# A code path of its own for the last 129 to 160 rows of the largest expert, in an attention and mixture-of-experts kernel

## The chip, the cores and the metric

The kernel is one program on one core of a Trainium2 chip. The metric is the device time of one execution in microseconds. Before the change the median of three runs is 644.22 us (641.96 to 645.08).

## The reference

Three layers follow each other on 2304 tokens of width 512, all in float32: masked attention, one dense layer with a softmax-gated activation and a normalisation, and a mixture of eight experts of which each token uses one. The change touches only the third:

```python
def _moe2_ref(x, modality_id, w_gate, modality_bias, w1, w2):
    logits = x @ w_gate + modality_bias[modality_id]
    e_idx = np.argmax(logits, axis=1)
    logits_s = logits - logits.max(-1, keepdims=True)
    probs = np.exp(logits_s)
    probs /= probs.sum(-1, keepdims=True) + 1e-09
    gate_w = probs[np.arange(N), e_idx]
    for e in range(E):
        mask = e_idx == e
        h = np.maximum(x[mask] @ w1[e], 0.0)
        out[mask] = gate_w[mask, None] * (h @ w2[e])
```

Here `w1` is 8 x 512 x 1024 and `w2` is 8 x 1024 x 512. How many rows (tokens) an expert gets is known only on the chip, from the router's result. With the inputs of the runs the reference gives the eight experts 0, 0, 9, 0, 0, 4, 111 and 2180 rows; of the first 1536 tokens 1462 go to the expert with 2180.

## The kernel before, in words

**The order of the work.** Attention and the dense layer write the rows of the third layer's input to `y_d` in DRAM, and a router sorts the experts by size. The largest is the main expert (index 0), the others follow. Two pieces of 256 rows of the main expert run early, from the first twelve of the eighteen 128-token tiles (`EARLY_T`). The rest of its rows are counted in `n_r[0]`, 2180 - 512 = 1668 here, and run in pieces of 256, numbered j: piece 0 to 5 hold 256 rows each, piece 6 the last 132. Pieces 0 to 2 run between the small experts (`main_step`, `small`), pieces 3 to 6 in `rest(3)`, the last function of the program. All matrix products split a number into a high part (rounded float32, names ending in H) and a low part (L), and add three products: high x high, high x low, low x high.

**One piece of 256 rows, `chunk256` (L1040 ff).** The input rows are already gathered by GpSimd (`gather`, L982), transposed by TensorE (`transpose_x`, L134) and lie as `gH` and `gL`, 512 x 256, with the rows along the columns (the profile calls them xTH and xTL). The *up* part is 96 matmuls on L1055: 8 pieces of 128 of the 1024 hidden features x 4 chunks of the 512 inputs x 3 products. The stationary operand is a 128 x 128 tile of `w1`, the moving one 256 columns of the rows. After each 24 matmuls ScalarE (L1061, relu into `hH`) and VectorE (L1062, the low part into `hL`) empty a PSUM tile of 2 x 256 columns. Then `expert_out` runs once for each half of the rows, an *output block* of 128 rows: 8 chunks of the hidden features x 3 products = 24 matmuls on L1015, with 128 rows of `hH` or `hL` as the stationary operand and 512 columns of `w2` moving. ScalarE multiplies the sum by the rows' gate values (L1020), and GpSimd scatters the block's rows to their places in the output tensor (L1021, an indirect DMA; rows beyond the count have an index out of range and are dropped). Between the two blocks `then` transposes the rows of the next piece, whose gathers `ahead` has issued at the piece's start.

**Which code a piece runs (`rest`, `level`, L1284 to L1309).** The levels are nested branches on `n_r[0]`, taken on every engine. Level j asks whether rows are left (L1290, more than 256 j) and whether more than 128 are left (L1291). If so it runs `chunk256`, also when only 129 of the 256 rows exist; otherwise `chunk_few` (L1081), which is written for up to 128 rows.

**How the small experts end.** `chunk_few` closes its output in one of two ways. Up to 64 rows (`tiny`): the sum comes in two halves of 64 partitions, ScalarE copies one (L1153), VectorE multiplies the other (L1154) and adds the copy (L1155). Up to 128 rows: ScalarE does 256 of the columns (L1157), VectorE twice 128 (L1159). Either is followed by one scatter (L1160).

**What sets the order.** Each engine runs its instructions in the order of the program; a scheduler orders them when the program is built. Scatters and gathers are issued by GpSimd's queue, one after the other, and two scatters to `out` in one piece of code are ordered by the framework where they name the same tensor.

Of the kernel before, what the change touches and what calls it, by code (L numbers as in the profile page):

```python
# [28 lines left out]
def tile_attention_moe_moe2(  # L29
# [38 lines left out]
    HALF = DM // 2  # L68
    YA = HALF + NE
    TINY = P // 2  # L70
    EARLY = 2
    EARLY_T = 12
    NTC = NTILE + 2 * EARLY
# [966 lines left out]
    def chunk256(w, idx, j, side=(), ahead=None, then=None, loads=()):  # L1040
# [37 lines left out]
            then()  # L1078
        expert_out(w, idx, 2 * j + 1, slice(P, 2 * P), step, (1, 4))

    def chunk_few(w, idx, j, side=(), then=None, blk=0, tiny=False):  # L1081
        wH1, wL1, wH2 = w[:3]
        step, last = stepper(side)
# [63 lines left out]
            last[0] = then()  # L1147
        down(2)
        down(3)
        o = yo[0:n_, 0]  # L1150
        gate = idx[0:n_, 2 * j, 1:2].bitcast(F32)
        if tiny:
            nc.scalar.copy(yo[0:TINY, 1], p[TINY:])  # L1153
            nc.vector.tensor_scalar(o, p[0:TINY], gate, None, ALU.mult)  # L1154
            nc.vector.scalar_tensor_tensor(o, yo[0:TINY, 1], gate, o, ALU.mult, ALU.add)  # L1155
        else:
            nc.scalar.activation(o[:, 0:256], p[:, 0:256], AF.Copy, scale=gate)  # L1157
            for s_ in (slice(256, 384), slice(384, 512)):
                nc.vector.tensor_scalar(o[:, s_], p[:, s_], gate, None, ALU.mult)  # L1159
        nc.gpsimd.indirect_dma_start(  # L1160
            out=out[:, :], out_offset=indirect(idx[0:n_, 2 * j, 2:3].bitcast(U32)),
            in_=o, in_offset=None, bounds_check=NT - 1, oob_is_err=False)

    state = None
    done_att = False
# [104 lines left out]
    def more_chunks(w, i, j, cap, x, gathered=False):  # L1270
        if j >= cap:
            return
        with tc.If(n_r[i] > 256 * j):
# [7 lines left out]
            with big.Else():  # L1281
                chunk_few(w, idx[i], j)

    def rest(j, gathered=True):  # L1284
        cap = NT // 256

        def level(j, now, later, ready):
            if j >= cap:
                return
            with tc.If(n_r[0] > 256 * j):  # L1290
                with tc.If(n_r[0] > 256 * j + P) as big:  # L1291
                    def ahead():
                        if not ready:
                            gather(now, idx[0], j + 1)
                        if j + 2 < cap:
                            gather(later, idx[0], j + 2)

                    def then():
                        transpose_x(now)

                    if j + 1 < cap:
                        chunk256(W[0], idx[0], j, (), ahead, then)
                    else:
                        chunk256(W[0], idx[0], j)
                    level(j + 1, later, now, True)
                with big.Else():
                    chunk_few(W[0], idx[0], j)

        level(j, *xg, gathered)  # L1309

# [120 lines left out]
```

## Time and profile before

| | |
|---|---|
| median of three runs | 644.22 us |
| profiled execution | 643.14 us, its span in the trace 641.4 us |
| granted TensorE clock, mean | 0.986 of full speed |
| TensorE matmul (PE) busy | 602.3 us, 94% of the span |
| TensorE weight load (PEld) | 535.7 us, 84% |
| VectorE (DVE) | 346.8 us, 54% |
| ScalarE (ACT) | 286.3 us, 45% |
| GpSimd (POOL) | 151.5 us, 24% |
| the up matmuls of `chunk256` (L1055), all nine pieces | 3 x 288 matmuls, 81.8 + 82.0 + 81.4 us busy |
| the scatters of `chunk256` (L1021) | 14 shown, 14.1 us of GpSimd |

The busy times come from the hardware profiler on the core. Matmuls are pipelined: one begins before the end of the one ahead, so the length of a record (284 ns for 256 columns) is more than the distance from one start to the next. That distance is what counts for the time of a stream, and it is read from the start times in the list of instructions. A few records are missing from the trace (L1055 shows 864 matmuls, which is 9 x 96, and L1021 shows 14 of 18 scatters).

### The profile page before, as it was taken

How to read it: one execution, taken by the hardware profiler on the slowest of the kernel's cores; microseconds unless marked ns; L12 is line 12 of the kernel's file. 1: busy time of each engine (PE TensorE's matmuls, PEld its weight loads, DVE VectorE, ACT ScalarE, POOL GpSimd, SP SyncE). 2: the span in 40 equal slices, each digit the busy share in tenths (PEclk: the TensorE clock that was granted, in tenths of full speed). 3: DMA queues.
4: the chain of work that ended last, by engine and by line, in shares of the span. 5: the costliest groups of instructions: out<-in, count | busy, mean ns of one | idle time of the engine just before them, and what ended most of it. 6: DMA issues, size and time to landing. Idle time of an engine off the chain costs nothing. (4 is left out here: it accounts for less than half of the span.)

```text
span 641.4 us, 14417 instructions
## 1 busy us (share of the span) xinstructions
PE 602.3 (94%) x5546; PEld 535.7 (84%) x5546; DVE 346.8 (54%) x1020; ACT 286.3 (45%) x673; POOL 151.5 (24%) x223
## 2 busy tenths in 40 slices
PE   5887989999999999999999999999899999999992
PEld 4765777998889988978889999989798888899891
DVE  4865887488556775577488743217264643120120
ACT  3646675555554566557265522124335352221210
POOL 3652432112112352011023312310111203112101
PEclk9997989999999999999999999999999999999997
DMA  8676630224312123110044301445455453012010
GB/s 224 189 179 171 158 108 19 54 56 117 82 55 57 53 59 108 37 36 17 18 149 148 98 19 34 112 158 158 143 165 198 147 187 104 17 50 66 33 34 25
DMA packets 48387, 61.64 MB, mean 96 GB/s; under 512 B 29313, under 2 KB 32923, under 8 KB 48285
## 3 DMA queue, kind: packets, MB, share of 16 engines
q1 hardware_dynamic: 41421, 44.09, 24.7%
q0 software_dynamic: 4272, 11.57, 5.8%
q10 hardware_dynamic: 2592, 4.72, 2.0%
q8 instruction: 52, 0.85, 0.6%
q14 instruction: 50, 0.41, 0.2%
HBM read 48.40 MB, written 10.26 MB: 91 GB/s over the span
## 5 line engine op out<-in xcount | busy, mean ns | idle before, releaser
L1015 PE MATMUL py<-w2H,winL 128*128 128x512 f32 x288 | 92.1, 395 | 0.0
L1055 PE MATMUL pf<-xTL,w1H 128*128 128x256 f32 x288 | 81.8, 284 | 1.0 <-DVE xTL L994 1.0
L1055 PE MATMUL pf<-xTH,w1H 128*128 128x256 f32 x288 | 82.0, 285 | 0.0
L1055 PE MATMUL pf<-xTH,w1L 128*128 128x256 f32 x288 | 81.4, 283 | 0.0
L1062 DVE SCALAR_TENSOR_TENSOR winL<-pf,winL 128x512 fp32r<-128x512 f32 x36 | 24.9, 692 | 95.9 <-ACT winL L1061 95.8
L628 PE MATMUL ph<-winH,xTH 128*128 128x512 f32 x144 | 58.8, 408 | 4.2 <-DVE so L643 3.1
L1015 PEld LDWEIGHTS py<-w2H,winL 128*128 128x128 f32 x288 | 53.4, 188 | 10.5
L1061 ACT ACTIVATE winL<-pf 128x512 fp32r<-128x512 f32 x36 | 21.6, 599 | 87.5 <-PE pf L1055 87.5
L1055 PEld LDWEIGHTS pf<-xTL,w1H 128*128 128x128 f32 x288 | 56.2, 195 | 1.9 <-DVE xTL L994 1.6
L628 PE MATMUL ph<-winL,xTH 128*128 128x512 f32 x144 | 57.6, 400 | 0.0
L1055 PEld LDWEIGHTS pf<-xTH,w1H 128*128 128x128 f32 x288 | 56.1, 195 | 1.0 <-issue 0.5
L628 PE MATMUL ph<-winH,xTL 128*128 128x512 f32 x144 | 56.9, 401 | 0.0
L1055 PEld LDWEIGHTS pf<-xTH,w1L 128*128 128x128 f32 x288 | 56.2, 195 | 0.0
L1021 POOL DMA_INDIRECT out_dram<-yo,idx x14 | 14.1, 1007 | 142.6 <-ACT yo L1020 124.4
L687 PE MATMUL pa<-woH,nH 128*128 128x264 f32 x144 | 42.3, 293 | 1.0 <-ACT nH L676 1.0
L687 PE MATMUL pa<-woH,nL 128*128 128x264 f32 x144 | 42.6, 296 | 0.0
L687 PE MATMUL pb<-woH,nH 128*128 128x256 f32 x144 | 41.2, 286 | 0.0
L687 PE MATMUL pb<-woH,nL 128*128 128x256 f32 x144 | 41.0, 284 | 0.0
L687 PE MATMUL pa<-woL,nH 128*128 128x264 f32 x144 | 40.9, 284 | 0.0
L687 PE MATMUL pb<-woL,nH 128*128 128x256 f32 x144 | 40.8, 283 | 0.0
L462 POOL TENSOR_TENSOR ex<-ex,rd 72x288 f32<-72x288 f32 (+2 forms) x32 | 22.3, 696 | 70.9 <-DVE rd L457 44.4
L628 PEld LDWEIGHTS ph<-winH,xTH 128*128 128x128 f32 x144 | 27.4, 191 | 10.6 <-DVE so L643 4.5
(288 smaller groups left out, 1535.7 us busy)
## 6 DMA issues: line engine op xcount, KB each, us to landing
raw<-in_moe_w_dram SPq DMA_DIRECT2D x36, 512.0 KB
y_d<-yt ACTq DMA_DIRECT2D x18, 256.0 KB
raw<-in_moe_w_in_dram SPq DMA_DIRECT2D x8, 512.0 KB
raw<-in_moe_w_out_dram SPq DMA_DIRECT2D x8, 512.0 KB
qn<-in_q_dram SPq DMA_DIRECT2D x8, 288.0 KB
kn<-in_k_dram SPq DMA_DIRECT2D x8, 288.0 KB
vn<-in_v_dram SPq DMA_DIRECT2D x8, 288.0 KB
qn<-in_q_dram SPq DMA_DIRECT2D x16, 144.0 KB
```

The costliest lines, as they stand in the source:

```text
L462: nc.gpsimd.tensor_tensor(ex, ex, rd.unsqueeze(2).to_broadcast([nq, nt, nk]), ALU.mult)
L628: nc.tensor.matmul(ph, a[:, c, ts_], w[:, c, cs], start=n == 0, stop=n == 3 * KD - 1)
L687: nc.tensor.matmul(p, a[:, f], w[:, f, cols], start=n == 0, stop=n == 3 * KF - 1)
L1015: nc.tensor.matmul(p, a[:, f, s], x, start=n == 0, stop=n == 3 * KF - 1)
L1021: nc.gpsimd.indirect_dma_start(out=out[:, :], out_offset=indirect(idx[:, col, 2:3].bitcast(U32)), in_=o, in_offset=None, bounds_check=NT - ...
L1055: mm = nc.tensor.matmul(p[:, u], a[:, c, fs], x[:, c], start=n == 0, stop=n == 3 * KD - 1)
L1061: last[0] = (nc.scalar.activation(hH[:, f2s], p, AF.Relu), nc.vector.scalar_tensor_tensor(hL[:, f2s], p, 0.0, hH[:, f2s].bitcast(F32), ALU ...
L1062: nc.vector.scalar_tensor_tensor(hL[:, f2s], p, 0.0, hH[:, f2s].bitcast(F32), ALU.max, ALU.subtract))
```

## The change

A level whose rows number 129 to 160 (`TAIL`) runs a new function, `chunk_tail`, and no longer `chunk256`.

- Its up matmuls move 160 columns in place of 256, into the same PSUM tiles. ScalarE's relu works on 160 columns; VectorE writes the low part of the first 128 rows into `hL` as before and that of the other 32 behind the 160 columns of `hH`.
- The first output block keeps its 24 matmuls. The second, of up to 32 rows, has 16: per chunk of hidden features one with 64 stationary columns (32 rows high, the same 32 rows low) against the high part of `w2`, and one with 32 stationary columns (high) against its low part. The 16 stand between the two halves of the first block's 24.
- The second block's sum comes in two halves of 32 partitions and is closed by `add_two`: ScalarE copies one half, VectorE multiplies the other by the gate and adds the copy, into a buffer in `hid`. The first block is closed by `scale_split` (ScalarE 256 columns, VectorE twice 128). Each ends with a scatter, `add_two`'s first.
- `add_two` and `scale_split` are also what `chunk_few` now ends with; the tiny form stages its sum in `hid` where it used `yo`.
- In the levels the inner branch asks for more than 160 rows first, and falls through to `chunk256`; the other side asks for more than 128 (`chunk_tail`) or runs `chunk_few`. Each piece of 256 rows gives a hint for the next level's branch at its start (`hint_tail`).
- `chunk_tail` gathers and transposes no next piece.

```diff
--- before.py
+++ after.py
@@ -68,6 +68,8 @@
     HALF = DM // 2
     YA = HALF + NE
     TINY = P // 2
+    EXTRA = P // 4
+    TAIL = P + EXTRA
     EARLY = 2
     EARLY_T = 12
     NTC = NTILE + 2 * EARLY
@@ -1078,6 +1080,26 @@
             then()
         expert_out(w, idx, 2 * j + 1, slice(P, 2 * P), step, (1, 4))
 
+    def scatter_rows(o, idx, col, n):
+        nc.gpsimd.indirect_dma_start(
+            out=out[:, :], out_offset=indirect(idx[0:n, col, 2:3].bitcast(U32)),
+            in_=o, in_offset=None, bounds_check=NT - 1, oob_is_err=False)
+
+    def scale_split(idx, col, p):
+        o, gate = yo[:, 0], idx[:, col, 1:2].bitcast(F32)
+        nc.scalar.activation(o[:, 0:256], p[:, 0:256], AF.Copy, scale=gate)
+        for s_ in (slice(256, 384), slice(384, 512)):
+            nc.vector.tensor_scalar(o[:, s_], p[:, s_], gate, None, ALU.mult)
+        scatter_rows(o, idx, col, P)
+
+    def add_two(idx, col, p, n):
+        o = hid.rearrange("p q f -> p (q f)")[0:n, 0:2 * DM].rearrange("p (u d) -> p u d", u=2)
+        gate = idx[0:n, col, 1:2].bitcast(F32)
+        nc.scalar.copy(o[:, 1], p[n:2 * n])
+        nc.vector.tensor_scalar(o[:, 0], p[0:n], gate, None, ALU.mult)
+        nc.vector.scalar_tensor_tensor(o[:, 0], o[:, 1], gate, o[:, 0], ALU.mult, ALU.add)
+        scatter_rows(o[:, 0], idx, col, n)
+
     def chunk_few(w, idx, j, side=(), then=None, blk=0, tiny=False):
         wH1, wL1, wH2 = w[:3]
         step, last = stepper(side)
@@ -1147,19 +1169,47 @@
             last[0] = then()
         down(2)
         down(3)
-        o = yo[0:n_, 0]
-        gate = idx[0:n_, 2 * j, 1:2].bitcast(F32)
         if tiny:
-            nc.scalar.copy(yo[0:TINY, 1], p[TINY:])
-            nc.vector.tensor_scalar(o, p[0:TINY], gate, None, ALU.mult)
-            nc.vector.scalar_tensor_tensor(o, yo[0:TINY, 1], gate, o, ALU.mult, ALU.add)
+            add_two(idx, 2 * j, p, TINY)
         else:
-            nc.scalar.activation(o[:, 0:256], p[:, 0:256], AF.Copy, scale=gate)
-            for s_ in (slice(256, 384), slice(384, 512)):
-                nc.vector.tensor_scalar(o[:, s_], p[:, s_], gate, None, ALU.mult)
-        nc.gpsimd.indirect_dma_start(
-            out=out[:, :], out_offset=indirect(idx[0:n_, 2 * j, 2:3].bitcast(U32)),
-            in_=o, in_offset=None, bounds_check=NT - 1, oob_is_err=False)
+            scale_split(idx, 2 * j, p)
+
+    def chunk_tail(w, idx, j):
+        wH1, wL1, wH2 = w[:3]
+        for f2 in range(KF // 2):
+            p = ps.tile([P, 2, 256], F32, name="pf", tag="h")[:, :, 0:TAIL]
+            for u in range(2):
+                fs = slice(f2 * 256 + u, f2 * 256 + 256, 2)
+                n = 0
+                for c in range(KD):
+                    for a, x in ((wH1, gH), (wH1, gL), (wL1, gH)):
+                        nc.tensor.matmul(
+                            p[:, u], a[:, c, fs], x[:, c, 0:TAIL], start=n == 0, stop=n == 3 * KD - 1)
+                        n += 1
+            f2s = slice(2 * f2, 2 * f2 + 2)
+            nc.scalar.activation(hH[:, f2s, 0:TAIL], p, AF.Relu)
+            for dst, r in ((hL[:, f2s, 0:P], slice(0, P)), (hH[:, f2s, TAIL:TAIL + EXTRA], slice(P, TAIL))):
+                nc.vector.scalar_tensor_tensor(
+                    dst, p[:, :, r], 0.0, hH[:, f2s, r].bitcast(F32), ALU.max, ALU.subtract)
+        p = ps.tile([P, DM], F32, name="py", tag="y")
+        p2 = ps.tile([P, DM], F32, name="py", tag="y")
+
+        def down(f):
+            fl = dict(stop=f == KF - 1, skip_group_check=True)
+            nc.tensor.matmul(p, hH[:, f, 0:P], wH2[:, f], start=f == 0, **fl)
+            nc.tensor.matmul(p, hH[:, f, 0:P], lo2(w, f), start=False, **fl)
+            nc.tensor.matmul(p, hL[:, f, 0:P], wH2[:, f], start=False, **fl)
+
+        for f in range(KF // 2):
+            down(f)
+        for f in range(KF):
+            fl = dict(stop=f == KF - 1, skip_group_check=True)
+            nc.tensor.matmul(p2[0:2 * EXTRA], hH[:, f, P:P + 2 * EXTRA], wH2[:, f], start=f == 0, **fl)
+            nc.tensor.matmul(p2[0:EXTRA], hH[:, f, P:TAIL], lo2(w, f), start=False, **fl)
+        for f in range(KF // 2, KF):
+            down(f)
+        add_two(idx, 2 * j + 1, p2, EXTRA)
+        scale_split(idx, 2 * j, p)
 
     state = None
     done_att = False
@@ -1281,6 +1331,10 @@
             with big.Else():
                 chunk_few(w, idx[i], j)
 
+    def hint_tail(j):
+        tc.mark_branch_hint_location(
+            f"tail{j}", n_r[0] > 256 * j + TAIL, engines=mybir.ALL_ENGINES)
+
     def rest(j, gathered=True):
         cap = NT // 256
 
@@ -1288,7 +1342,7 @@
             if j >= cap:
                 return
             with tc.If(n_r[0] > 256 * j):
-                with tc.If(n_r[0] > 256 * j + P) as big:
+                with tc.If(n_r[0] > 256 * j + TAIL, preferred_fallthrough_block=True, label=f"tail{j}") as big:
                     def ahead():
                         if not ready:
                             gather(now, idx[0], j + 1)
@@ -1299,12 +1353,16 @@
                         transpose_x(now)
 
                     if j + 1 < cap:
+                        hint_tail(j + 1)
                         chunk256(W[0], idx[0], j, (), ahead, then)
                     else:
                         chunk256(W[0], idx[0], j)
                     level(j + 1, later, now, True)
                 with big.Else():
-                    chunk_few(W[0], idx[0], j)
+                    with tc.If(n_r[0] > 256 * j + P, preferred_fallthrough_block=True) as some:
+                        chunk_tail(W[0], idx[0], j)
+                    with some.Else():
+                        chunk_few(W[0], idx[0], j)
 
         level(j, *xg, gathered)
 
```

On GpSimd's queue the last piece (level 6 of `rest(3)`) read so before; xg_5954 is the buffer for a next piece's rows, and the names in brackets are what an instruction waits for (DMASW: the landing of an earlier indirect DMA).

```order
L1290 COMPARE_AND_BRANCH
L1291 COMPARE_AND_BRANCH
L982 DMA xg_5954<-y_d,idx_5945 128x512 [waits DMASW6_49,PE_49]
L982 DMA xg_5954<-y_d,idx_5945 128x512 [waits DMASW7_49,PE_49]
L1021 DMA out_dram<-yo,idx_5945 2304x512 [waits DMASW5_49,Activation_49]
L1021 DMA out_dram<-yo,idx_5945 2304x512 [waits DMASW0_49,Activation_49]
L1290 COMPARE_AND_BRANCH
```

With the change the same place, level 6's `chunk_tail`, reads:

```order
L1362 COMPARE_AND_BRANCH
L1084 DMA out_dram<-hid,idx_5945 2304x512 [waits DMASW7_49,DMASW6_49,DVE_49]
L1084 DMA out_dram<-yo,idx_5945 2304x512 [waits DMASW0_49,DMASW7_49,DVE_49,Activation_49]
L1345 ISA [waits DMASW4_49,DMASW5_49,DMASW3_49,DMASW6_49,DMASW2_49,DMASW1_49]
L1362 UNCONDITIONAL_BRANCH
```

The two gathers are gone. The second block's scatter (from `hid`) now comes first, and the first block's scatter (from `yo`), the last one of the program, waits for VectorE, for ScalarE and for DMASW7, which is the landing of the scatter ahead of it; before, the last scatter waited for ScalarE and for a DMA of an earlier time.

On TensorE's queue the new piece begins with the first four rows; the first two matmuls, which read the transposed rows, wait for PE's own count, ScalarE and VectorE. The last two rows are the last pair of 64 and 32 stationary columns.

```order
L1362 COMPARE_AND_BRANCH
L1186 MATMUL pf<-xTH,w1H 128x160 [waits PE_49,Activation_49]
L1186 MATMUL pf<-xTL,w1H 128x160 [waits DVE_49]
L1186 MATMUL pf<-xTH,w1L 128x160
...
L1207 MATMUL py<-w2H,winL 64x512 [waits DVE_49,Activation_49]
L1208 MATMUL py<-xTL,winL 32x512
```

The 96 up matmuls are followed by 12 of the first block, the 16 of 64 and 32 stationary columns, and 12 of the first block; the eight transposes that stood between the two blocks are not there.

## Rows read from the trace of the kernel before

**Rows 1.** Busy time by stretch, last piece: us, PE, PEld, DVE, ACT, POOL, PEclk, DMA, GB/s

```profile
605.78:629.30 23.52, 23.52 (x153) 21.12 (x151) 4.06 (x6) 4.84 (x8) 4.00 (x4) 1.00 0.16 47
```

**Rows 2.** Instructions in order of time, last piece: start us, us, engine, line, operation

```profile
605.78 0.28 PE L1055 MATMUL pf<-xTH,w1H 128*128 128x256 f32 x1
...
611.41 0.28 PE L1055 MATMUL pf<-xTH,w1L 128*128 128x256 f32 x1
...
612.21 0.71 PE L134 MATMUL px<-ident,xg 128*128 128x128 f32 x5
...
627.32 0.39 PE L1015 MATMUL py<-xTL,winL 128*128 128x512 f32 x1
...
628.91 0.39 PE L1015 MATMUL py<-w2H,winL 128*128 128x512 f32 x1
629.38 0.69 ACT L1020 ACTIVATE yo<-py,idx 128x512 f32<-128x512 f32 x1 [3.17 <-PEq L1290]
630.35 1.01 POOL L1021 DMA_INDIRECT out_dram<-yo,idx  x1 [2.83 <-ACTq L1290]
```

**Rows 3.** DMA queues from 620 to 642 us: packets, MB, share of 16 engines

```profile
q0 software_dynamic: 160, 0.27, 3.4%
```

**Rows 4.** Two lines' instructions at the end: count, min/median/max ns, first and last start

```profile
L1290 POOLq INC_SWDGE_SEM  x1: 1480/1480/1480, 630.7 to 630.7; - x1
```

```profile
L1426 POOLq DRAIN  x3: 46/109/5450, 635.1 to 641.1; - x3
```

**Rows 5.** The router in order of time, and weight loads by shape (busy us, mean ns)

```profile
111.91 1.03 PE L286 MATMUL pg<-wg,wt 128*128 128x8 f32 x8
```

```profile
L1055 PEld LDWEIGHTS pf<-xTH,w1L 128*128 128x128 f32 x288 | 56.2, 195 | 0.0
...
L134 PEld LDWEIGHTS px<-ident,xg 128*128 128x128 f32 x68 | 8.5, 140 | 2.1
L286 PEld LDWEIGHTS pg<-wg,wt 128*128 128x128 f32 x64 | 7.9, 192 | 0.8 <-ACT wt L283 0.4
```

**Rows 6.** A tiny expert's last matmuls, in order of time

```profile
534.60 0.40 PE L1126 MATMUL py<-woH,winL 128*128 128x512 f32 x1
534.84 0.39 PE L1128 MATMUL py<-woL,winL 128*64 128x512 f32 x1
```

**Rows 7.** The tiny expert's closing, in order of time, with idle time and releaser

```profile
535.31 0.58 ACT L1153 COPY yo<-py 64x512 f32<-64x512 f32 x1 [0.38 <-PE py L1128]
...
536.70 0.75 DVE L1155 SCALAR_TENSOR_TENSOR yo<-yo,idx 64x512 f32<-64x512 f32 x1
...
538.25 0.93 POOL L1160 DMA_INDIRECT out_dram<-yo,idx  x1 [2.72 <-DVE yo L1155]
```

**Rows 8.** Chain of waits from 600 us: the landings of two first-block scatters

```profile
603.13 2.73 DMA out_dram<-yo,idx
...
626.49 3.02 DMA out_dram<-yo,idx
```

**Rows 9.** Closing of the small expert of 111 rows, in order of time

```profile
467.01 0.40 PE L1131 MATMUL py<-woH,winL 128*128 128x512 f32 x1
...
467.44 0.47 ACT L1157 ACTIVATE yo<-py,idx 128x256 f32<-128x256 f32 x1 [0.30 <-DMA xg<-y_d,idx]
467.95 0.61 DVE L1159 TENSOR_SCALAR yo<-py,idx 128x128 f32<-128x128 f32 x2
```

```profile
469.37 1.02 POOL L1160 DMA_INDIRECT out_dram<-yo,idx  x1 [1.61 <-issue]
```

**Rows 10.** Branches on TensorE's queue: count, min/median/max ns, first and last start

```profile
L1290 PEldq COMPARE_BRANCH  x1: 65/65/65, 601.7 to 601.7; - x1
```

```profile
L1290 PEldq COMPARE_BRANCH  x6: 65/68/4557, 533.0 to 629.5; - x6
```

```profile
L1383 PEldq COMPARE_BRANCH  x4: 84/442/458, 452.1 to 532.5; - x4
```

**Rows 11.** Attention's plain float32 score matmuls, in order of time

```profile
121.31 0.68 PE L427 MATMUL bank<-kz,qT 128*72 128x72 f32 x8
```

## The prediction

> **What bounds the kernel now.** I read four views of the profile before the change, in this order. First the busy time by stretch: over the last piece, 605.78 to 629.30 us, TensorE is busy all 23.52 us at a granted clock of 1.00 while VectorE and ScalarE work 4 to 5 us of it [rows 1]. So in this piece a matmul saved is time saved, up to the point where the closing work takes over. Second the instructions in order of time [rows 2]: the first up matmul starts at 605.78, the 48th at 611.41, so one starts every 5.63 / 47 = 0.1198 us; the 512-column ones at the end follow each other at (628.91 - 627.32) / 7 = 0.227 us. The last starts at 628.91, the eviction on ScalarE at 629.38, the last scatter at 630.35: 1.44 us from the start of the last matmul to the scatter that ends the work. Third the DMA traffic of the end: from 620 us on the software queue moves 0.27 MB [rows 3]. The two scatters write rows of 2,048 bytes; 128 rows are 0.262 MB, so the second block holds about 4 rows (0.265 to 0.275 MB would be 129.4 to 134.3 rows in both blocks). This fits the 132 rows that the reference's routing leaves, and it lies inside 129 to 160: the new code will run, once, at the end. Fourth what follows the last scatter: GpSimd's closing instruction of 1.48 us and its drain of 5.45 us [rows 4], part of the 641.40 - 630.35 = 11.05 us after the scatter's start. Every engine ran this ending before and will run it after; I leave it at 11.05 us. What counts is therefore the start of the last scatter.
>
> **The change, part by part.** *Up matmuls.* There are still 96, each with a new 128 x 128 stationary tile, now over 160 columns in place of 256. By columns alone one would cost 0.1198 - 96 x (0.227 - 0.1198) / 256 = 0.080 us: the lower bound. But each needs its own weight load. The router's matmul records (plain float32, each with its own load) move only 8 columns and still start every (1.03 - 0.256) / 7 = 0.111 us; their loads take 192 ns in the profile, those of the up matmuls 195 ns, those of the PE transposes 140 ns [rows 5] (0.256 us is the length of one such matmul record). Same load length, hence the same floor, I take it: 0.111 us. The upper bound is a stream at the rate of the kernel's plain float32 matmuls, 0.289 us (second rival). I take 0.111, the row with the like load, between these far ends, so 96 x (0.1198 - 0.111) = 0.84 us saved where the column count promises 3.8.
>
> *Second output block.* 24 matmuls of 512 columns become 16, with 64 and 32 stationary columns. A pair of a 128-column and a 64-column one in the small expert's code starts 0.24 us apart [rows 6]; I take 0.235. So 24 x 0.227 - 16 x 0.235 = 1.69 us saved.
>
> *Transposes.* The old piece transposes the rows of a next piece that does not exist: 8, of which five in a row take 0.71 us [rows 2]; with their edges they hold the stream for 0.96 us (23.13 us from first to last matmul start, less 96 x 0.1198 and 47 x 0.227). They go, and so do two gathers on GpSimd and four evictions, which lay beside TensorE's work and cost nothing there.
>
> Together the last matmul starts 0.84 + 1.69 + 0.96 = 3.49 us earlier: 96 x 0.111 + 12 x 0.227 + 16 x 0.235 + 11 x 0.227 = 19.64 us after the first, against 23.13.
>
> *Closing work.* This is where I see a new wait. Let T be the start of the last second-block matmul; 0.235 + 11 x 0.227 = 2.73 us later starts the last matmul of all. The second block is now closed by a copy on ScalarE, a multiply and a multiply-add on VectorE in turn, and a scatter. The small expert does just this: from its last matmul's start at 534.84 to the end of the multiply-add at 537.45 pass 2.61 us [rows 6, 7]. Those rows have 64 partitions, the new ones 32, of the same 512 elements; I keep the time. With the 0.28 us that a scatter needs after its last producer (eviction done at 630.07, scatter at 630.35 [rows 2]), the second block's scatter starts at T + 2.89. The first block's scatter stands behind it on GpSimd and waits for its landing, since both write the output tensor; such landings take 2.73 and 3.02 us at the ends of the last two pieces [rows 8]. I take 2.8: T + 5.69. Then, as in the small experts' code where a separate wait stands ahead of the scatter, 0.80 us (537.45 to 538.25 [rows 7]; 468.56 to 469.37 [rows 9]), against at least 0.28: T + 6.49, or 3.76 us after the last matmul's start. Even without the landing, the split eviction (ScalarE on 256 columns, then VectorE on twice 128) takes 469.37 - 467.01 = 2.36 us in the 128-row code [rows 9], so its halves run in turn and the closing is not shorter than the old 1.44. The loss is 3.76 - 1.44 = 2.32 us; its bounds are 3.14 and 3.96 in place of 3.76 (landing of 2.7 or 3.0, issue 0.28 or 0.80).
>
> *Branches and hints.* Each level of the rest adds a register operation and a prefetch hint on every engine; TensorE's queue runs ahead and hides them. The last piece is now reached by a taken jump. TensorE's queue comes to this place at 601.7, 4.1 us before its matmuls are through. Hinted branches of the same kind took 442 ns at the median, an unhinted far jump up to 4,557 ns [rows 10]. The jump is hinted one piece ahead, so I set it at nothing, covered by those 4.1 us; unhinted it would stick out by 0.5. All other code keeps its order on every engine; that the tiny experts now stage their sum in another buffer moves no instruction.
>
> *Sum.* -3.49 + 2.32 = -1.17 us. The profiled execution took 643.14 us (span 641.4), 1.08 below the median of the three runs, 644.22. So I expect 641.97 for a like execution and **643.0 us** in the median, 0.2% less. By my reading a measurement of this kernel tells 0.5%, 3.2 us, from no change; three runs before lie 3.1 us apart.
>
> **The rivals.** *Columns set the pace (10%).* If loads hide fully behind matmuls, 160 columns cost 0.080 us and the up section saves 3.0 us more: 643.0 - 3.0 = 640.0 us, faster by 0.65%. For it speaks that the 256- and 512-column rows follow the columns [rows 2]; against it the 8-column rows at 0.111 us [rows 5]. [...]
>
> *A short moving operand falls to the plain float32 rate (30%), the other side.* The score matmuls on plain float32 operands leave two records each, 8 records of 72 columns in (0.68 - 0.228) / 7 = 0.065 us steps [rows 11], so 0.130 us per 72 columns or 0.289 per 160. For it speaks that every rounded-float32 stream of this trace moves 256 columns or more [rows 2], and that every row with fewer is on plain operands: the fast rate is never seen under 256 columns, and the new code is the first to try. In width, 160 lies as far from the slow 72 as from the fast 256. Against it: operands, stationary tiles and loads are those of the 256-column row, and I see in the rows no reason why the operand's type should count at one width and not at the other. I give it nearly a third. The price is 96 x (0.289 - 0.111) = 17.1 us: 660.1 us. It decides from 0.111 + 1.17 / 96 = 0.123 us per matmul; above that the gain is gone, above 0.157 the kernel is slower by over 0.5%.
>
> *The jump is not covered (6%).* If the hint fails, TensorE stands 0.5 us; if both the jump and the branch behind it fetch anew, about 4.6 us more, 643.0 + 5.1 = 648.1. Against it: the hinted rows [rows 10].
>
> *The landing does not hold up the last scatter (3%).* Then the closing takes 2.36, not 3.76 us: 641.6, still within 0.5%. That the new code does not run at all is excluded by [rows 3] well enough (under 1%; then 644.2).
>
> **How the numbers follow.** My forecast has 50%, and its own range is 641.3 to 644.7: the bounds of the closing and the second block, and half the spread of the runs. The plain float32 rate holds 30%, so the full range must reach it: down to 640.5, which leaves most of the first rival out, and up to the plain float32 rate with 0.9 us for the spread, 661.0. Faster by over 0.5%: the first rival and the lower edge of the forecast's spread (3 in 100), 0.13. Slower by over 0.5%: the second rival, half of the third and one in a hundred besides, 0.34. The rest, 0.53, is no change.
>
> **What would show it.** In the profile after, up matmuls of 160 columns should start 0.11 us apart; at 0.08 the first rival holds, above 0.123 the second. The second block's scatter should start about 2.9 us after its last matmul's start, and GpSimd should idle before the last scatter on a DMA's landing, not on ScalarE. The last matmul should start near 625.4, the last scatter near 629.2. A gap on TensorE before the first 160-column matmul would be the jump. If the last scatter moves by 3 us or more with the up matmuls at 0.11, my closing is wrong.

## The result, and the profile after

The changed kernel takes **652.52 us** in the median of 11 runs (649.72 to 655.35), against 644.38 us for the kernel before (11 runs). The ratio is 1.0104 with a 95% interval of 1.0071 to 1.0137: slower by about 1%, where 0.2% less was forecast. The profiled execution took 653.15 us, its span is 651.2.

In the last piece each part came to within 0.6 us of the prediction; most of the loss stands 160 us ahead of it. The two traces, cut where the same matmuls start (the small experts are the ones of 111, 9 and 4 rows):

| stretch | before, us | after, us | difference |
|---|---|---|---|
| start to the first up matmul of the 111-row expert | 454.11 | 452.99 | -1.12 |
| that expert, up to the next `chunk256` (475.15 after) | 13.13 | 22.16 | **+9.03** |
| on to the first up matmul of the 9-row expert | 23.55 | 22.95 | -0.60 |
| on to that of the 4-row expert | 33.89 | 34.70 | +0.81 |
| on to piece 3 (545.26 after) | 10.38 | 12.46 | **+2.08** |
| pieces 3 to 5 | 70.72 | 71.67 | +0.95 |
| last piece, first to last matmul | 23.13 | 20.26 | **-2.87** |
| last matmul to last scatter | 1.44 | 3.58 | **+2.14** |
| last scatter to the end | 11.05 | 10.43 | -0.62 |
| sum: the span | 641.40 | 651.20 | +9.80 |

The first row's -1.12 us says little: two profiles of the kernel before (run 11 is the second) differ there by 1.89 us, 454.11 against 456.00.

Busy time by stretch of the kernel after: the 111-row expert, the 9-row one with its neighbours, up to piece 3, pieces 3 to 5, the last piece, its closing (us, then PE, PEld, DVE, ACT, POOL, PEclk, DMA share, GB/s):

```profile
452.99:475.15 22.16, 15.19 (x89) 13.55 (x89) 3.40 (x8) 4.52 (x11) 3.89 (x4) 0.85 0.18 63
475.15:509.84 34.69, 33.51 (x221) 29.88 (x221) 17.56 (x25) 14.80 (x25) 5.91 (x6) 1.00 0.51 168
509.84:545.26 35.42, 33.50 (x220) 29.89 (x221) 19.09 (x26) 14.80 (x25) 7.17 (x6) 1.00 0.55 165
545.26:616.93 71.67, 71.67 (x456) 65.54 (x457) 12.47 (x19) 13.83 (x23) 11.82 (x12) 0.98 0.14 43
616.93:637.19 20.26, 20.26 (x137) 17.56 (x135) 3.71 (x10) 3.02 (x6) 1.01 (x1) 1.00 0.05 16
637.19:640.77 3.58, 0.39 (x2) 0.00 (x0) 0.61 (x2) 0.47 (x1) 0.90 (x2) 1.00 0.05 11
```

In the first of these TensorE is busy 15.19 of 22.16 us at a clock of 0.85; before, the same stretch had no idle time and a clock of 1.00, and ScalarE's first write to `hid` waited for TensorE alone:

```profile
454.11:467.24 13.13, 13.13 (x88) 11.87 (x89) 2.46 (x6) 4.01 (x10) 3.39 (x4) 1.00 0.22 78
```

```profile
455.88 0.39 ACT L1101 ACTIVATE hid<-pq 128x256 f32<-128x256 f32 x1 [3.17 <-PE pq L1100]
```

What TensorE waits for after the change, in the instructions in order of time:

```profile
457.00 0.28 PE L1120 MATMUL pq<-winH,xTH 128*128 128x256 f32 x1
457.81 0.98 POOL L1023 DMA_INDIRECT out_dram<-yo,idx  x1 [6.92 <-issue]
...
462.94 0.66 ACT L1123 ACTIVATE hid<-pq 128x256 f32<-128x256 f32 x2 [10.88 <-DMA out_dram<-yo,idx]
463.38 0.70 PE L136 MATMUL ph<-ident,hid 128*128 128x128 f32 x2 [6.11 <-ACT hid L1123]
...
464.31 0.41 PE L1120 MATMUL pq<-winH,xTH 128*128 128x256 f32 x1
464.52 0.41 PE L1121 MATMUL pq<-winH,xTL 128*128 128x256 f32 x1
```

TensorE waits 6.11 us for ScalarE's write to `hid`. The row puts ScalarE's own wait down to the scatter out of `yo` that GpSimd issued at 457.81, rows of the piece before, with which this expert has nothing to do. That scatter cannot have ended the wait: it had landed 2.7 us after its issue, at 460.5, and ScalarE starts at 462.94. What ends just then is an instruction on GpSimd's queue, L1452, at the end of the branch that is skipped here (it is for a second expert of more than 128 rows or of none, and holds the first copy of the levels):

```profile
out_dram<-yo,idx POOLq DMA_INDIRECT x1, 2.7
```

```profile
L1452 POOLq INC_SWDGE_SEM  x1: 860/860/860, 461.9 to 461.9; - x1
```

It moves the counters of the indirect DMAs (DMASW) on, for the DMAs of the skipped branch as I take it; the trace shows the moves alone. The counters DMASW1 to DMASW7 move at 462.67 to 462.72, and ScalarE's first semaphore instruction runs at 462.71; in runs 2, 3 and 5, which have the same wait, the two lie as close together. So ScalarE waits until GpSimd has come past the skipped branch.

Afterwards 256-column matmuls start 0.21 us apart, against 0.12 before:

```profile
457.28:463.38 6.10, 0.00 (x0) 0.00 (x1) 0.00 (x0) 0.44 (x2) 0.98 (x1) 0.75 0.11 46
463.38:467.20 3.82, 3.82 (x18) 3.82 (x19) 0.42 (x1) 1.07 (x4) 0.99 (x1) 0.51 0.22 66
```

After 6.10 us without a matmul the granted clock is 0.51 for 3.82 us. From the first transposes to the first 512-column matmul TensorE now takes 3.85 us (463.38 to 467.23), and took 2.16 before (458.19 to 460.35): the low clock costs 1.7 us. From the expert's first up matmul to those transposes it takes 10.39 us in place of 4.08, 6.3 more; with 1.0 us up to the next `chunk256` this makes the 9.0 us of the table.

That last 1.0 us and the other gaps are a second loss: TensorE's queue at the ends of the small experts (branches on the label of the next expert; count, min/median/max ns, first and last start):

```profile
L1441 PEldq COMPARE_BRANCH  x4: 82/3211/3837, 451.5 to 540.7; - x4
```

The three at the ends took 3.30, 3.12 and 3.84 us; before, 0.46, 0.44 and 0.44 [rows 10]. They leave TensorE idle for 0.86, 1.18 and 1.92 us, and behind the last of them the clock is 0.64 over 4.74 us:

```profile
509.84 0.37 PE L1057 MATMUL pf<-xTH,w1H 128*128 128x256 f32 x1 [1.18 <-ACT hid L1098]
...
545.26 0.37 PE L1057 MATMUL pf<-xTH,w1H 128*128 128x256 f32 x1 [1.92 <-DVE hid L1099]
```

```profile
545.26:550.00 4.74, 4.74 (x27) 4.74 (x28) 0.31 (x1) 0.00 (x0) 1.88 (x2) 0.64 0.09 26
```

And the last piece, the answer to [rows 1, 2, 8]:

```profile
616.93 0.24 PE L1186 MATMUL pf<-xTH,w1H 128*128 128x160 f32 x1
...
628.08 0.28 PE L1186 MATMUL pf<-xTH,w1L 128*128 128x160 f32 x1
...
634.44 0.40 PE L1208 MATMUL py<-xTL,winL 128*32 128x512 f32 x1
...
637.19 0.39 PE L1201 MATMUL py<-w2H,winL 128*128 128x512 f32 x1
637.28 0.90 POOL L1084 DMA_INDIRECT out_dram<-hid,idx  x1 [18.12 <-DVE hid L1100]
...
640.77 0.98 POOL L1084 DMA_INDIRECT out_dram<-yo,idx  x1 [2.59 <-DMA out_dram<-hid,idx]
```

```profile
637.28 2.69 DMA out_dram<-hid,idx
```

The 160-column matmuls start (628.08 - 616.93) / 95 = 0.117 us apart. The last scatter waits for the landing of the one ahead of it.

### The profile page after: what moved, and what is told of

It is laid out like the page before. It is cut to its first block, busy times and chain, and to the rows that moved or that the text cites. A ratio compares the mean times of both kernels' runs of the same rounds, so it can differ in the third digit from the quotient of the medians.

```text
span 651.2 us, 14415 instructions
## 1 busy us (share of the span) xinstructions
PE 602.7 (93%) x5530; PEld 535.4 (82%) x5530; DVE 348.1 (53%) x1026; ACT 284.1 (44%) x671; POOL 147.1 (23%) x221
## 5 line engine op out<-in xcount | busy, mean ns | idle before, releaser
L1017 PE MATMUL py<-w2H,winL 128*128 128x512 f32 x256 | 81.8, 395 | 0.0
L1057 PE MATMUL pf<-xTH,w1H 128*128 128x256 f32 x256 | 73.7, 289 | 4.0 <-DVE hid L1099 1.9
L1057 PE MATMUL pf<-xTH,w1L 128*128 128x256 f32 x256 | 73.1, 286 | 0.0
L1057 PE MATMUL pf<-xTL,w1H 128*128 128x256 f32 x256 | 73.1, 285 | 0.0
L1064 DVE SCALAR_TENSOR_TENSOR winL<-pf,winL 128x512 fp32r<-128x512 f32 x32 | 22.1, 692 | 83.2 <-ACT winL L1063 83.1
L1057 PEld LDWEIGHTS pf<-xTH,w1H 128*128 128x128 f32 x256 | 50.7, 198 | 5.6 <-issue 2.4
L1017 PEld LDWEIGHTS py<-w2H,winL 128*128 128x128 f32 x256 | 47.4, 188 | 9.3
L1063 ACT ACTIVATE winL<-pf 128x512 fp32r<-128x512 f32 x32 | 19.2, 599 | 81.5 <-PE pf L1057 79.5
L1057 PEld LDWEIGHTS pf<-xTL,w1H 128*128 128x128 f32 x256 | 50.7, 198 | 0.3
L1057 PEld LDWEIGHTS pf<-xTH,w1L 128*128 128x128 f32 x256 | 50.6, 198 | 0.0
```

The costliest lines, as they stand in the source:

```text
L1017: nc.tensor.matmul(p, a[:, f, s], x, start=n == 0, stop=n == 3 * KF - 1)
L1057: mm = nc.tensor.matmul(p[:, u], a[:, c, fs], x[:, c], start=n == 0, stop=n == 3 * KD - 1)
L1063: last[0] = (nc.scalar.activation(hH[:, f2s], p, AF.Relu), nc.vector.scalar_tensor_tensor(hL[:, f2s], p, 0.0, hH[:, f2s].bitcast(F32), ALU ...
L1064: nc.vector.scalar_tensor_tensor(hL[:, f2s], p, 0.0, hH[:, f2s].bitcast(F32), ALU.max, ALU.subtract))
```

## The experiments

Two theories. **A:** the scatter out of `hid` adds a wait to the next writer of `hid`. The order of ScalarE's instructions with their waits shows it. The first write to `hid` in the 111-row expert's code read before and after the change:

```
L1101 ACTIVATE hid<-pq 128x256 [waits PE_49,Activation_49] x2
```
```
L1123 ACTIVATE hid<-pq 128x256 [waits DMASW3_49,DMASW1_49,DMASW5_49,DVE_49,DMASW7_49,PE_49,Activation_49]
```

Four DMASW names are new. They are counters of indirect DMAs: in the trace after, the landing of the scatter issued at 457.81 moves one on at 460.33 to 460.50, and GpSimd's L1452 moves DMASW1 to DMASW7 on at 462.67 to 462.72. **B:** the jumps are slow, because of the new hints, or (**B2**) because of where the code now lies. Some edits below need the same small means: `add_two` takes its buffer as an argument.

**Run 1, no scatter out of `hid`.**

```diff
-            add_two(idx, 2 * j, p, TINY)
+            add_two(idx, 2 * j, p, TINY, yo[0:TINY])
...
-        add_two(idx, 2 * j + 1, p2, EXTRA)
+        o, gate = yo[0:EXTRA, 1], idx[0:EXTRA, 2 * j + 1, 1:2].bitcast(F32)
+        nc.scalar.copy(o, p2[EXTRA:2 * EXTRA])
+        nc.vector.tensor_scalar(o, o, gate, None, ALU.mult)
+        nc.vector.scalar_tensor_tensor(o, p2[0:EXTRA], gate, o, ALU.mult, ALU.add)
+        scatter_rows(o, idx, 2 * j + 1, EXTRA)
```

> Edit: no scatter reads hid any more; the tiny experts stage in yo again, and the last piece builds its second block in place in one half of yo. Theory A (hid): in the changed kernel ScalarE's first write to hid in the expert of 111 rows waited for the landing of an older scatter, because the code of the last piece scatters out of hid. Then the gap of 6.4 us on TensorE before that expert's first transposes goes, and the stretch of slow matmuls behind it with it: the time from that expert's first up matmul to the next small expert's falls from 45.1 us to about 37.6 (36.7 in the kernel before, plus about 0.9 of a slow jump), in all about 645 us. Rival (the gap is a code fetch or a late gather): the gap stays and the time is 652 within 1.5.

Measured: 647.07 us, ratio to the kernel before 1.0040 (1.0008 to 1.0072). In order of time, and TensorE's branches:

```profile
456.28 0.39 ACT L1124 ACTIVATE hid<-pq 128x256 f32<-128x256 f32 x1 [4.20 <-PE pq L1123]
```

```profile
L1446 PEldq COMPARE_BRANCH  x4: 82/3420/4147, 451.6 to 537.3; - x4
```

ScalarE waits for TensorE alone, and the gap is gone. Theory A holds; but from the 111-row expert's first up matmul to the next small expert's it took 41.1 us, not 37.6, since the jump took 4.15 us here, left a gap of 1.8 us and a clock of 0.58 for the 4 us behind it.

**Run 2, only the tiny experts back in `yo`** (the first edit of run 1 alone).

> Edit: only the tiny experts stage in yo again; the last piece still scatters its second block out of hid. Theory A puts the wait down to the last piece's code, a copy of which stands ahead of the small experts in the program and never runs here: the gap of 6.4 us stays, 652 us within 1.5. Rival A2: it is the tiny experts' own scatter out of hid: the gap goes, about 645 us, as in the run without any scatter out of hid.

Measured: 654.14 us, 1.0122 (1.0048 to 1.0196).

```profile
463.54 0.66 ACT L1124 ACTIVATE hid<-pq 128x256 f32<-128x256 f32 x2 [10.22 <-DMA out_dram<-yo,idx]
```

The wait is still there: it comes from the last piece's code, not from the tiny experts. (The time is 0.6 us above the expected bound; two of the jumps took 3.5 and 4.4 us here.)

**Run 3, no hints.**

```diff
-                        hint_tail(j + 1)
```

> Edit: the hint for the next level is left out. Theory B (hints): the jumps of TensorE at the ends of the small experts, 3.3, 3.1 and 3.8 us long against 0.44 to 0.46 before, are slow because of the new hints. Then they fall to about 0.45 us and some 4 us come back: 648. Rival B2 (where the code lies): the hints have no part, the jumps stay over 3 us or change without a pattern, 652 within 2. Either way the jump into the last piece is unhinted: TensorE reaches it about 4 us ahead of its matmuls, so a gap of at most 0.5 us is expected there.

Measured: 651.99 us, 1.0104 (1.0071 to 1.0136).

```profile
L1440 PEldq COMPARE_BRANCH  x4: 89/3118/3238, 452.2 to 540.7; - x4
```

The jumps stay at 3.0 to 3.2 us: not the hints.

**Run 4, old code ahead of the small experts.** The call of `rest` that stands there is for the case in which every other expert is empty.

```diff
-            rest(1, False)
+            rest(1, False, False)
```

(The third argument keeps the old levels: `chunk256` above 128 rows, no hints, no `chunk_tail`.)

> Edit: the copy of the levels that stands ahead of the small experts keeps the old code (no last-piece function, no hints); the levels behind the small experts are as in the change. Theory A: no code ahead of the small experts scatters out of hid, so the wait of the 111-row expert and its gap go: about 645 us at most. Theory B2: TensorE's code up to the small experts is as long as in the kernel before, so if the place of the code decides, the jump at the end of the 111-row expert returns to about 0.45 us and the sum to 641 to 642.5: the last piece by itself is about 1.4 us shorter than before from its first matmul to the end of the span. Rival (hints decide): the jumps stay slow, 645.

Measured: 643.83 us, 0.9982 (0.9947 to 1.0016); the profiled execution 641.25.

```profile
L1446 PEldq COMPARE_BRANCH  x4: 82/441/2452, 451.7 to 531.7; - x4
```

```profile
625.36 0.39 PE L1201 MATMUL py<-w2H,winL 128*128 128x512 f32 x1
625.45 0.90 POOL L1084 DMA_INDIRECT out_dram<-hid,idx  x1 [18.25 <-DVE hid L1100]
...
629.10 0.98 POOL L1084 DMA_INDIRECT out_dram<-yo,idx  x1 [2.75 <-DMA out_dram<-hid,idx]
```

No wait, no gap over 0.7 us behind the expert's first matmul, jumps two and three at 0.44 us. With the loss upstream gone, the change is worth what its last piece is worth: a difference that this measurement cannot tell from nothing, as forecast. The median lies 1.3 us above the 642.5 that was expected here at most, and the first jump, at 2.45 us, did not come back, though it left no gap.

**Run 5, the new code only where it never runs.** The copy of the levels ahead of the small experts is new, every level that runs is old, the tiny experts stage in `yo`. On the changed kernel, with run 2's edit and the third argument of run 4, this is:

```diff
-            rest(i - 1)
+            rest(i - 1, True, False)
```

> Edit, to the kernel before: only the copy of the levels that stands ahead of the small experts, which never runs with these inputs, gets the new code of the last piece (staging in hid) and its hints; every level that runs keeps the old code, and the tiny experts stage in yo. Theories A and B2: the wait of the 111-row expert and the slow jumps are both there though no new instruction runs: the gap of 4 to 6 us, jumps over 3 us, and with the old last piece 652 to 654 us. Rival (the loss needs the new code to run): 644.5 within 1.5.

Measured: 653.77 us, 1.0147 (1.0116 to 1.0178).

```profile
460.93 0.66 ACT L1124 ACTIVATE hid<-pq 128x256 f32<-128x256 f32 x2 [10.06 <-DMA out_dram<-yo,idx]
461.37 0.70 PE L136 MATMUL ph<-ident,hid 128*128 128x128 f32 x2 [5.21 <-ACT hid L1124]
```

The loss is there in full with code that is not executed once.

**Run 6, the same, its second block in `yo`** (run 5 with the second edit of run 1).

> Edit: as the last one, but the copy that never runs builds its second block in yo and scatters nothing out of hid. Theory A: no gap at the 111-row expert's first transposes. Theory B2: TensorE's three jumps still take over 3 us, since the code that lies ahead of them is as long: 647 to 650 us. If B2 is wrong they take 0.45 us and the time is 644.5 within 1.5.

Measured: 649.63 us, 1.0075 (1.0039 to 1.0111).

```profile
455.04 0.38 ACT L1124 ACTIVATE hid<-pq 128x256 f32<-128x256 f32 x1 [2.74 <-PE pq L1123]
```

```profile
L1451 PEldq COMPARE_BRANCH  x4: 84/3207/3801, 451.7 to 532.9; - x4
```

No wait, but all three jumps at 3.0 to 3.8 us: B2. Code that lies ahead and never runs makes the kernel 0.75% slower, and with the wait of run 5 by 1.5%. The profiled execution is the fastest of run 6's seven, 644.61 us; the jumps left gaps of 0.52, 1.42 and 1.68 us in it. That the jumps make up the whole 0.75% of the median is not shown.

**Run 7, one eviction** (on run 4):

```diff
-        scale_split(idx, 2 * j, p)
+        nc.scalar.activation(yo[:, 0], p, AF.Copy, scale=idx[:, 2 * j, 1:2].bitcast(F32))
+        scatter_rows(yo[:, 0], idx, 2 * j, P)
```

> Edit, to the kernel with old code ahead of the small experts (which took 643.8): the first block of the last piece is emptied by one ScalarE instruction of 512 columns, as before the change, in place of three. Theory (the landing ends last): the last scatter waits for the landing of the second block's scatter, so a shorter eviction changes nothing: 3.7 us from the last matmul to the last scatter within 0.3, 643.8 within 1. Rival (the eviction ends last): the last scatter comes 0.9 us earlier, 1.44 to 2.8 us after the last matmul.

Measured: 643.78 us, 0.9991 (0.9965 to 1.0017).

```profile
626.09 0.39 PE L1201 MATMUL py<-w2H,winL 128*128 128x512 f32 x1
626.18 0.90 POOL L1084 DMA_INDIRECT out_dram<-hid,idx  x1 [18.12 <-DVE hid L1100]
626.57 0.69 ACT L1212 ACTIVATE yo<-py,idx 128x512 f32<-128x512 f32 x1 [2.21 <-PE py L1201]
629.84 0.99 POOL L1084 DMA_INDIRECT out_dram<-yo,idx  x1 [2.76 <-issue]
```

The eviction is over at 627.26, the scatter starts at 629.84, 3.75 us after the last matmul as in run 4: the landing ends last, not the eviction.

**Run 8, the second block's matmuls written first** (on run 7):

```diff
-        for f in range(KF // 2):
-            down(f)
         for f in range(KF):
...
-        for f in range(KF // 2, KF):
+        add_two(idx, 2 * j + 1, p2, EXTRA)
+        for f in range(KF):
             down(f)
-        add_two(idx, 2 * j + 1, p2, EXTRA)
```

> Edit: as the last one, and the 16 matmuls of the second block with their closing stand ahead of all 24 of the first block. Then the second block's scatter has landed before the first block is done (its last matmul is 24 x 0.227 = 5.4 us ahead of the last of all, its scatter lands about 5.7 us after it), and the last scatter comes 1.4 us after the last matmul, as before the change, or 1.8 at most: 2 to 2.3 us less than with old code ahead of the small experts, 641.6 us, which is 0.5% under the kernel before. If the landing has no part, the gain is 0.9 us as in the last run's rival.

Measured: 643.36 us, 0.9988 (0.9965 to 1.0011), a miss.

```profile
629.11 0.90 POOL L1084 DMA_INDIRECT out_dram<-hid,idx  x1 [17.93 <-DVE hid L1100]
...
629.48 0.39 PE L1201 MATMUL py<-w2H,winL 128*128 128x512 f32 x1
...
632.57 0.98 POOL L1084 DMA_INDIRECT out_dram<-yo,idx  x1 [2.56 <-issue]
```

Written first is not placed first: the scheduler put the last four of the 16 behind ten matmuls of the first block, the second block's scatter came 0.37 us before the last matmul, and the last scatter 3.1 us after it.

**Run 9, the new code only in the copies from the running one onward** (on run 4).

```diff
-                rest(i - 1)
+                rest(i - 1, True, i >= 4)
```

> Edit: only the copies of the levels from the one that runs here onward get the last piece's code; every copy ahead of them keeps the old one. Theory B2 (place): with old code ahead of the small experts alone, TensorE's first jump still took 2.45 us, since a copy of the levels that the jump passes over had grown. Now the code ahead of and at all three jumps is as long as before the change, so the three take 0.44 to 0.46 us, and no gap over 0.7 us stands on TensorE behind the first matmul of the 111-row expert. Last piece as in the run with old code ahead of the small experts: 24.1 us from its first matmul to the last scatter, 20.3 us to the last matmul. Time 643.5 within 1, about 1 us under the kernel before. Rival (the first jump depends on when the fetch starts, not on the place): it takes 2 us or more again.

Measured: 642.92 us, 0.9989 (0.9953 to 1.0025).

```profile
L1446 PEldq COMPARE_BRANCH  x4: 89/390/3262, 451.1 to 531.8; - x4
```

Jumps two and three stay short, the first took 3.26 us with a gap of 1.1 us behind it, though the code ahead of it and up to its target is as long as before the change. For the first jump, place as I had put it is not the cause.

**Run 10, both edits, held in order** (run 9 with run 8's order and eviction):

```diff
+            if f == 0:
+                queue_after(mm, last)
```

(`mm` is the first block's first matmul, `last` the second block's last.)

> Edit: as the last one, with one ScalarE eviction for the first block, and with all 16 matmuls of the second block held ahead of the first of the first block's 24 (in the earlier run with this edit the scheduler had put the last four of them only 14 matmuls before the end, and the second block's scatter came 0.4 us before the last matmul). Theory (the landing ends last): the second block's scatter is out 2.5 us before the last matmul, lands at about the last matmul, and the last scatter comes 1.4 to 1.8 us after the last matmul, against 3.1 and 3.7: about 22 us from the piece's first matmul to the last scatter, 641.5 us, 0.4 to 0.5% under the kernel before. Rival (the landing has no part, GpSimd's issue is slow by itself): 3 us again, 643.

Measured: 641.77 us, 0.9958 (0.9925 to 0.9992).

```profile
624.32 0.90 POOL L1084 DMA_INDIRECT out_dram<-hid,idx  x1 [15.33 <-DVE hid L1100]
...
626.96 0.39 PE L1203 MATMUL py<-w2H,winL 128*128 128x512 f32 x1
627.43 0.69 ACT L1212 ACTIVATE yo<-py,idx 128x512 f32<-128x512 f32 x1 [4.94 <-PE py L1203]
628.39 0.98 POOL L1084 DMA_INDIRECT out_dram<-yo,idx  x1 [3.17 <-ACT yo L1212]
```

The last scatter comes 1.43 us after the last matmul and waits for ScalarE. The time is 0.4% under the kernel before, and the whole interval lies below 1.

**Run 11, the kernel before, profiled again.**

> Edit: none; the kernel before, profiled a second time. In the runs whose code ahead of the small experts is as before, TensorE's second and third jump took 0.34 to 0.45 us, but the first 1.06 to 3.9 us, where the one profile of the kernel before shows 0.46. Theory (the first jump varies from execution to execution, with the start of its code fetch): 1 us or more here is as likely as 0.46, with the second and third at 0.44. Rival (the first jump is 0.46 whenever all code behind it is old): 0.46 again.

One execution, 644.93 us.

```profile
L1384 PEldq COMPARE_BRANCH  x4: 84/440/461, 454.5 to 534.4; - x4
```

0.46 us again, as the rival says. Two of two profiles of the old kernel have a short first jump; none of the six with new code behind the small experts alone has.

**Run 12, run 10 again.**

> Edit: none against the run with the second block held first and new code only in the last copies; a second measurement. Expected: 0.3 to 0.6% under the kernel before, the last scatter 1.4 us after the last matmul, jumps two and three at 0.44 us, the first anywhere from 0.46 to 4 us.

Measured: 641.46 us, 0.9946 (0.9918 to 0.9975). Its jumps are 1.65, 0.44 and 0.44 us.

## Why the prediction was wrong

- **The step that failed:** "All other code keeps its order on every engine; that the tiny experts now stage their sum in another buffer moves no instruction." Both halves are true, and neither is enough. The change added no work there but a wait: ScalarE's first write to `hid` must now wait for the counters of indirect DMAs, because a scatter out of `hid` stands in the code ahead of it, in a branch that does not run; on the path that runs, GpSimd brings the counters up to date only when its queue comes past that branch, at 462.7. It cost 6.3 us, and 1.7 us more at the low clock. I compared the order of the instructions and not what they wait for; the row with four new names was there to be read. And it is not the tiny experts' staging that did it (run 2), but `chunk_tail`'s (runs 1, 4 and 5).
- **The second failure:** "Each level of the rest adds a register operation and a prefetch hint on every engine; TensorE's queue runs ahead and hides them." I asked what the new code costs where it runs, not what it does to the rest. The jumps at the ends of three small experts, which I had used as my evidence that such branches take 442 ns [rows 10], became 3 to 4 us long. Run 6 shows that code which never runs does it. (The other gaps and the low clock behind them are in the +0.81, +2.08 and +0.95 us of the table.)
- **Up matmuls**, 0.111 us forecast: 0.117. The term was mis-sized by 96 x 0.006 = 0.6 us of a 3.49 us saving; the measured one is 2.87. The rival of the columns (0.080) is out, and so is that of the plain float32 rate (0.289): at 160 columns this stream is nearly as slow as at 256 (0.1198), and no slower. The full range held the time only because of that second rival, so for a reason that did not occur.
- **Second block**: 0.235 us forecast for each of its 16 matmuls, (634.67 - 630.98) / 16 = 0.231 measured, the matmul at 634.67 being the first behind them.
- **Closing**: 3.76 us after the last matmul forecast, 3.58 measured, 3.74 in run 4. The second block's scatter started 637.28 - 634.44 = 2.84 us after its last matmul (2.89), landed in 2.69 (2.8), and the last one waited for it, as run 7 and run 10 confirm from both sides. Of the change's own parts this was right, and it took back most of what the matmuls gained.
- **The jump into the last piece** was covered: no gap stands ahead of 616.93, and run 3 without hints shows none either. But it was no jump of 442 ns. With its hint it took 3.34 us, in run 3 without one 3.33; it was hidden because it started 3.9 us before the piece's first matmul, and the hint did nothing that shows:

```profile
L1345 PEldq COMPARE_BRANCH  x1: 3342/3342/3342, 613.0 to 613.0; - x1
```

- **The end** after the last scatter shrank by 0.62 us, which I had set at nothing. At least part of it goes with the new piece: the end takes 10.1 to 10.4 us in all ten profiles in which that ran, 10.7 in runs 5 and 6 with the old one, 10.9 and 11.1 in the two of the kernel before. Why was not found out.

Put together, -2.87 + 2.14 - 0.62 = -1.35 us came from the last piece and the end (forecast -1.17), and +11.15 us from ahead of them. That -1.35 lies so near to -1.17 is in part luck: the 0.62 us of the end make up for the 0.62 us by which the matmuls fell short.

What goes with the length of a jump shows in the queue q8, which the profile calls `instruction`: 52 packets of 16,384 bytes, 0.85 MB, in the kernel before as in the one after. I read each as a fetch of code. In the kernel before a fetch lies between 462.0 and 464.4 us (it begins at 462.29), ahead of the jump at 464.35; after the change there is none from 466 to 471.4, and one starts only at 472.01, during the jump that begins at 471.33:

```profile
q8 instruction: 1, 0.02, 2.5%
```

```profile
q8 instruction: 1, 0.02, 2.1%
```

(The queue's packets, MB and share, the first of the kernel before from 462 to 464.4 us, the second of the kernel after from 471.4 to 475.) The rows do not name the engine of a fetch, but the 42 jumps at the ends of small experts, three in each of the 14 profiles, leave little doubt. The 18 that took 0.46 us or less have a q8 fetch that began 1.96 to 5.06 us before them. The 24 longer ones have none so early: the fetch began between 1.26 us before the jump's start and 2.04 us after it, and the jump ended 1.32 to 1.52 us after the end of the fetch, however late that was. My reading of these 42: a jump is short when its code has been fetched ahead, and otherwise as long as the fetch is late, as at the first jump, 0.46 us before the change against 3.30 after. What code a fetch brings is not shown.

What stays open is why a fetch starts late. With more code ahead it did so at all three jumps (run 6, 3.0 to 3.8 us), and with the old code ahead the second and third were short again (0.34 to 0.45 us in runs 4, 7 to 10 and 12). But the first, with no new code ahead of it, in five kernels over six profiles, took 1.06 to 3.9 us where the kernel before takes 0.46: its fetch began from 1.26 us before to 1.60 us after the jump's start, against 2.06 and 1.96 us before it in the two profiles of the old kernel. Why it starts late in these six was not found out.

## What to carry to other kernels

Compare two programs by what each instruction waits for, not only by their order: here a buffer that a DMA now read made its next writer wait, though the DMA stood in a branch that was not taken (ScalarE idle for 10.9 us, in run 5 for 10.1); the writer waited until GpSimd, which issues those DMAs, had come past that branch. Code that never ran was not free either (0.75% in run 6); test a rare branch's price with a kernel that has it and never runs it. And when a closing step ends the work, first ask which landing it waits for (2.69 us here), then make the short block early and hold it there, since the scheduler did not keep the order in which it was written (run 8: 3.1 us from the last matmul to the last scatter, held in run 10: 1.43).

## What the runs showed of the hardware that I had not expected

- A rounded-float32 matmul of 160 columns with a fresh 128 x 128 tile starts every 0.117 us, one of 256 columns every 0.120: 37.5% fewer columns, 2% less time.
- After 6.1 us without matmuls the granted clock was 0.51 for the 3.8 us that followed. After shorter gaps it was low in some places (0.64 after 1.92 us, 0.58 after 1.77 us in run 1, each over the next 4 to 5 us) and 1.00 in others (after 1.68 us in run 6 from 537.21, after 1.56 us in run 8 from 471.03, after 2.17 us in the kernel before from 454.11): the length of the gap alone does not tell these apart.
- TensorE's jump at the end of a small expert took 0.34 to 0.46 us or 1.06 to 4.4 us, in all 14 profiles, and nothing between; the long ones ended 1.32 to 1.52 us after a fetch of 16,384 bytes on q8.
- In the kernel after, GpSimd spent at the end of the skipped branch 0.86 us on one instruction that moves the counters of the indirect DMAs on, and ScalarE, which waited for such counters, had stood idle for 10.9 us by then.
